# New addresses for the attention buffers, an early load of part of A12, and R21 in front of the other late loads

## The chip, the core and the metric

The kernel runs on one core of one Trainium2 chip. The core has five engines that work side by side and wait for each other through semaphores: TensorE (PE), which multiplies matrices, with its weight loads shown apart as PEld; VectorE (DVE); ScalarE (ACT); GpSimd (POOL), which in this kernel almost only issues DMAs; and SyncE (SP), which issues most of the DMAs. 16 DMA engines move the data between the large memory (HBM) and the core's own memory, which has 128 partitions.

The metric is the device time of one execution in microseconds (us), the median of several. The profile is of one more execution. Its span goes from its first instruction to its last.

## What is computed

Two branches work on the same x of 2048 rows and 1024 columns and are mixed, row by row, by a gate. Cut to what matters:

```python
x = A_x                                                  # (1, 2048, 1024), bf16
g = sigmoid((x * gate_w).sum(-1, keepdims=True))

# A: attention of 32 heads of 32; each row looks at 8 rows: itself and 2, 4, .. 14 before it
qkv = x @ wqkv                                           # 1024 x 3072
logits = einsum("bhsd,bhswd->bhsw", q, kg) * 32**-0.5    # kg, vg: the 8 rows of k, v
attn = softmax(where(mask, logits, -1e9))
a = einsum("bhsw,bhswd->bhsd", attn, vg) @ wo            # heads side by side, 1024 x 1024

# B: a gated feed-forward
h = gelu(x @ w_gate) * (x @ w_up)                        # 1024 x 3584, twice
b = h @ w_down                                           # 3584 x 1024

out = g * a + (1 - g) * b
```

## The kernel before

**Storage.** Nearly all of the core's memory is one tile, `arena`, of 200.5 KB in each partition. Everything in it has an address in KB, written by hand at the head of the file (`R_Q`, `R_O`, `R_BUF`, ...), and different stages use the same addresses one after the other. Semaphore waits are derived from these addresses: an instruction waits for earlier ones that read or wrote the bytes that it touches.

**Stages.** The rows are handled in two halves s of 1024, and each half in two chunks c of 512. First come `units`: products of 512 columns by Strassen-like schemes with seven products instead of eight (methods `p1` to `p4` of `Unit`, all matmuls at L364). The first units make q, k and v, the others gate and up, two pairs of columns at a time; each pair's h is multiplied together (L252, for the last two pairs also by 1 - g at L255) and stored to `h_d` by POOL (L258). `n` is the number of units, about 6 us each. While PE runs the units, DVE also does the attention: background tasks with priorities and wake times (`bg`, `run_bg`) are stepped after each unit with a budget of time. The order of every engine is thus fixed when the program is built.

**Attention output.** `pv_all` goes through the eight blocks of 256 rows in the order `PVO` = 0, 1, 2, 4, 5, 6, 3, 7; i is the turn, a the block. For each it has the weights in `ab_[i % 2]` (4 KB), v in `vb[i % 2]` (4.25 KB), multiplies them (L743) into `prod2` (two buffers of 8 KB), folds the products (L750) into `ob_[i % 2]` (4 KB) and stores that to `o_d` by POOL (L771). The loads of turn i + 1 are issued at the beginning of turn i. The last turn, i = 7, uses the buffers of index 1.

**Down projection.** After the units, `down(s)` multiplies the half's activations A (h of 14 pairs and the 4 tiles of the attention's output: NK = 18 tiles of 1 KB) by R (`w_down` and `wo`), again with seven products in place of eight, and most of these with a second level of the same (`level2`, matmuls at L1025; single-level products at L1050). `A11, A12, A21, A22` are the four parts of A (first digit: which 512 rows; second: which of the two tiles of a pair), `R11 .. R22` those of R, `T1 .. T4` are differences of R made early and kept in HBM (`t_d`). Each lies in one of ten 18 KB buffers, `bufs[k]` from 1 + 18k KB; for s = 0: A12 in buffer 2 (37 to 55 KB), A22 in 3 (55 to 73), A11 in 4, R11 in 5, A21 in 6 (109 to 127), R21 in 7 (127 to 145), T1 in 1 (19 to 37), T2 in 9.

For s = 0 the first half of `down` does, on PE: A11 by R11 (72 matmuls, L1050), A12 by R21 (72, L1050), then `level2` of S and T1 (126, L1025), `level2` of S2 and T2 (126, L1025), A12 by R22 (72, L1050). On DVE, in this order: the rest of the scaling by 1 - g (`scale_task`, L904, 4 tiles an instruction), S = A21 + A22 and AD = A11 - A21 (`comb_task`, L911), the forms L5 and R5 for the first `level2` (L986 and L994, woven), S2 (L911), the forms L6, three instructions of A12 - S2, the forms R6 (L994), and so on.

**The late loads of the first `down`.** `NE_` = 12 is the number of pairs whose h has not been scaled before it is stored, `KX` = 11, the number of tiles of A21 that fit below a buffer of the units at 120 KB. The loads of A are issued in parts:

- `pre_down_0`: A21's tiles 0 to 10; `pre_down_1`: A11's 12 tiles and its o tiles
- `pre_down_2`, called at the end of `pv_all`: A22's 12 tiles, then A12's 12 tiles, and a scaling task for each in this order
- `pre_down_3`, right after it: A21's twelfth tile and its o tiles, the o tiles of A22 and A12, and R21 (two DMAs: 14 tiles of `w_down`, 4 of `wo`, L827)
- `pre_down_4`: the tiles of the last two pairs, issued on POOL (L812)
- T1 and T2 (L830) after the last unit

All but `pre_down_4` go through SP, whose queue is in order: while one DMA waits for its buffer, the ones behind it are not issued. Each DMA takes one of eight semaphore lanes in turn and waits for the DMA eight before it in its lane.

Of the kernel before, what the change touches and what calls it, by code (L numbers as in the profile page):

```python
# [18 lines left out]
NWIN = 8  # L19
# [3 lines left out]
NJ = 4  # L23
SJ = AC // NJ
# [25 lines left out]
R_TF = (92, 100, 108)  # L50
R_TB = (16, 24)
R_S = (16, 24)
R_O = (32, 36)
R_VB = 40
R_AB = 49
R_PROD2 = 57
R_BUF = tuple(1 + 18 * k for k in range(10))
R_U2 = 181
R_QS = 189
# [1 line left out]
KV = AC + HALO  # L61


def _win_ap(src: bass.AP, dims):
    return AP(src.tensor, src.offset, [list(src.ap[0])] + [list(d) for d in dims])
# [3 lines left out]
def kernel(  # L69
# [20 lines left out]
    NT = KT  # L90
    NPAIR = Df // (2 * P)
    NK = NPAIR + NT // 2
    NBLK = S // AC
# [9 lines left out]
    def reg(kb, n):  # L103
        o = int(kb * KB)
        return arena[:, o:o + n]

    def reg3(kb, a, b):
        return reg(kb, a * b).rearrange("p (a b) -> p a b", a=a)

    def reg4(kb, a, b, c):  # L110
        return reg(kb, a * b * c).rearrange("p (a b c) -> p a b c", a=a, b=b)
# [12 lines left out]
    NE_ = NPAIR - 2  # L124
# [10 lines left out]
    with tc.manual_schedule(engines={mybir.EngineType.PE, mybir.EngineType.DVE, mybir.EngineType.Activation,  # L135
# [296 lines left out]
        def bg(gen, prio, wake):  # L432
            t = Task(gen, prio, wake)
            tasks.append(t)
            tasks.sort(key=lambda t_: t_.prio)
            return t
# [134 lines left out]

        qb = [reg3(R_Q + 9 * i, NT, AC) for i in range(2)]
        kb = [reg3(R_Q + 9 * i + 4, NT, KV) for i in range(2)]
        vb = [reg3(R_VB + 4.25 * i, NT, KV) for i in range(2)]
        pr_off = [R_PR + 4 * i for i in range(4)] + [R_PROD + 4 * i for i in range(2)]
        prod = [reg3(o, NWIN, AC) for o in pr_off]
        attn_all = reg3(R_ATTN, NBLK, SC)
        mask = reg3(R_MASK, NWIN, SJ)
        ab_ = [reg4(R_AB + 4 * i, NJ, NWIN, SJ) for i in range(2)]
        ob_ = [reg3(R_O[i], NT, AC) for i in range(2)]  # L580
        prod2 = [reg4(R_PROD2 + 8 * i, 2, NJ, NWIN * SJ) for i in range(2)]

# [133 lines left out]
        def pv_load(a, i):  # L716
            src = w_d[a].rearrange("h j n -> h (j n)")
            nc.sync.dma_start(out=ab_[i % 2].rearrange("p j w s -> p (j w s)"),
                              in_=AP(src.tensor, src.offset,
                                     [[NJ * SC, 32], [0, 4], [1, NJ * SC]]))  # L720
            nc.sync.dma_start(out=vb[i % 2], in_=v_d[:, :, a * AC:a * AC + KV])
# [3 lines left out]
        def pv_all():  # L725
            for k in (0, 1):
                while PVO[k] not in ready:
                    yield None
            pv_load(PVO[0], 0)
            yield None  # L730
            for i, a in enumerate(PVO):
                if i + 1 < NBLK:
                    while PVO[i + 1] not in ready:
                        yield None
                    pv_load(PVO[i + 1], i + 1)
                if i == 0:
                    pv_task[0].prio = 5
                    tasks.sort(key=lambda t_: t_.prio)
                    yield None
                v, ab, o_ = vb[i % 2], ab_[i % 2], ob_[i % 2]  # L740

                def mult(t):
                    TT(out=prod2[(t // 2) % 2][:, t % 2], in0=ab,  # L743
                       in1=_win_ap(v[:, t, HALO:HALO + AC], [[SJ, NJ], [-DIL, NWIN], [1, SJ]]), op=ALU.mult)

                def fold(t, w):
                    pr = prod2[(t // 2) % 2]
                    h = lambda k: pr[:, :, :, k * w * SJ:(k + 1) * w * SJ]
                    out_ = h(0) if w > 1 else o_[:, t:t + 2, :].rearrange("p t (j s) -> p t j s", j=NJ)
                    TT(out=out_, in0=h(0), in1=h(1), op=ALU.add)  # L750

                mult(0)
                yield 1.14
                mult(1)
                yield 1.14
                for t in range(0, NT, 2):
                    nxt = t + 2 < NT
                    if nxt:
                        mult(t + 2)
                        yield 1.14  # L760
                    fold(t, 4)
                    yield 1.14
                    if nxt:
                        mult(t + 3)
                        yield 1.14
                    fold(t, 2)
                    yield 0.68
                    fold(t, 1)
                    yield 0.4
                a0 = a % BPS % 2 * AC  # L770
                nc.gpsimd.dma_start(out=o_d[a // BPS][a % BPS // 2][:, :, a0:a0 + AC], in_=o_)  # L771
            while now[0] < n - 6:
                yield None
            pre_down_2(0)

        def late_forms():
# [24 lines left out]
        bg(spill(0), 4, QE + 2)  # L801
        bg(spill(1), 4, QE + 2)
        pv_task = [bg(pv_all(), 4.2, QE + 3)]

        bufs = [reg3(R_BUF[k], NK, SC) for k in range(10)]
        NH_ = NPAIR

        def load_A(b, s, half, c, i0, i1, with_o, eng=nc.sync):
            for e, (a, z) in enumerate(((i0, min(i1, NE_)), (max(i0, NE_), i1))):
                if z > a:  # L810
                    src = h_d[s][e][:, :, c * SC:(c + 1) * SC].rearrange("p (i two) s -> p i two s", two=2)
                    eng.dma_start(out=b[:, a:z, :], in_=src[:, a - e * NE_:z - e * NE_, half, :])  # L812
            if with_o:
                nc.sync.dma_start(out=b[:, NH_:NK, :], in_=o_d[s][c][:, half * 4:half * 4 + 4, :])
# [10 lines left out]
        def load_R(b, half, nh, i0=0, i1=NK):  # L825
            for sl, src in r_parts(half, nh, i0, i1):
                nc.sync.dma_start(out=b[:, sl, :], in_=src)  # L827

        def load_T(b, k):
            nc.sync.dma_start(out=b, in_=t_d[k - 1][:])  # L830
# [65 lines left out]
        def Bs(s):  # L896
            return {k: bufs[v] for k, v in plan[s].items()}

        def scale_task(b, s, c, ia, ib):
            t0 = s * SUP + c * SC  # L900
            om = omgrep[:, t0:t0 + SC].rearrange("p (o s) -> p o s", o=1)
            for i0 in range(ia, ib, 4):
                i1 = min(i0 + 4, ib)
                TT(out=b[:, i0:i1, :], in0=b[:, i0:i1, :], in1=om.to_broadcast([P, i1 - i0, SC]), op=ALU.mult)  # L904
                yield 0.05 + 0.273 * (i1 - i0)
# [28 lines left out]

        KX = int(R_P5A[0] - R_BUF[6])

        def load_o(s, *names):
            for k in names:
                load_A(Bs(s)[k], s, int(k[2]) - 1, int(k[1]) - 1, 0, 0, True)

        def pre_down_0(s):
            load_A(Bs(s)["A21"], s, 0, 1, 0, KX, False)
            bg(scale_task(Bs(s)["A21"], s, 1, 0, KX), 6, n - 2)

        def pre_down_2(s):
            pd["end"] = True
            for k, c in (("A22", 1), ("A12", 0)):
                load_A(Bs(s)[k], s, 1, c, 0, NE_, False)
                bg(scale_task(Bs(s)[k], s, c, 0, NE_), 7, n)
            if now[0] >= NX0 + 3:  # L950
                pre_down_3(s)

        def pre_down_3(s):
            load_A(Bs(s)["A21"], s, 0, 1, KX, NE_, True)
            load_o(s, "A22", "A12")
            loads(s, "R21")

        def pre_down_4(s):
            B = Bs(s)
# [3 lines left out]
        def loads(s, *names):  # L963
            B = Bs(s)
            for k in names:
                if k[0] == "A":
                    load_A(B[k], s, int(k[2]) - 1, int(k[1]) - 1, 0, NH_, True)
                elif k[0] == "R":
                    load_R(B[k], int(k[1]) - 1, int(k[2]) - 1)
                else:  # L970
                    load_T(B[k], int(k[1]))
# [173 lines left out]
        at(n - 10, lambda: pre_down_0(0))  # L1145
        at(n - 7, lambda: pre_down_1(0))
        at(NX0 + 3, lambda: pd.get("end") and pre_down_3(0))
        def run_last(b):
            now[0] = b
# [72 lines left out]
```

## Time and profile before

| | us |
|---|---|
| median of 3 runs | 735.02 (734.26 to 735.18) |
| the profiled execution | 733.06 |
| its span | 731.2 |
| PE busy | 717.2 |
| DVE busy | 655.0 |
| ACT busy | 317.3 |
| PE idle in all between its matmuls | about 10 |

The busy times are of the whole span, over stages that have different limits: an engine that is 98% busy over all can still stand still at one place. A line of the timeline gives start, length, engine, source line, operation, tiles written and read, and in brackets the engine's idle time before it and what ended it. DMA issues stand at the time at which SP or POOL issued them; a long issue means that the queue took it only after that time. The time from issue to landing comes from the DMA view of a narrow window.

For the stretch around the end of the units these landings are (from the DMA view; issue times from the timeline):

| DMA | KB | issued | us to landing |
|---|---|---|---|
| A22, 12 tiles (SP) | 1536 | 504.86 | 10.3 |
| last block's o_, store (POOL) | 512 | 505.13 | 8.2 |
| A12, 12 tiles (SP) | 1536 | 513.38 | 7.1 |
| A21, twelfth tile (SP) | 128 | 513.99 | 9.0 |
| R21, w_down (SP) | 1792 | 517.11 | 18.6 |
| R21, wo (SP) | 512 | 517.63 | 19.5 |
| T1 (SP) | 2304 | 529.20 | 15.0 |

### The profile page before, as it was taken

To read this page: it belongs to the slowest core of one execution; us is meant where nothing else is said; L and a number is where in the kernel's file an instruction comes from. 1 tells how busy PE (TensorE), PEld (TensorE's weight loads), DVE (VectorE), ACT (ScalarE), POOL (GpSimd) and SP (SyncE) were. 2 spreads that over 40 slices of the span, in tenths; PEclk is the share of its full clock that TensorE was granted. 3 is DMA by queue.
4 is the path that set the end of the run, shared out by engine and by line. 5 is a ranking of instruction groups with operands and counts; after the bars stand their busy time and mean duration, and the time that the engine had idled before them with its cause. 6 is when DMAs were issued, how large, how long until landed. Compare 5 with 4: busy or idle time off the path is not lost. (4 is left out here: it accounts for less than half of the span.)

```text
span 731.2 us, 10391 instructions
## 1 busy us (share of the span) xinstructions
PE 717.2 (98%) x3945; PEld 393.2 (54%) x3945; DVE 655.0 (90%) x703; ACT 317.3 (43%) x570; POOL 114.7 (16%) x212
## 2 busy tenths in 40 slices
PE   8999999999999999999999999999969999999998
PEld 4466666655544444444444444444437766758573
DVE  3699999999999999999999999999779798799944
ACT  4554445444557565555555555555112211232210
POOL 1233445143201210001000000101100011110001
PEclk9999999999999999999999999999989999999999
DMA  9967544287264834443364836533991976965401
GB/s 278 278 180 224 210 139 156 76 282 267 99 211 145 278 113 146 147 144 123 110 203 126 265 121 220 150 137 123 348 363 49 397 254 205 382 276 203 194 22 58
DMA packets 112610, 140.78 MB, mean 193 GB/s; under 512 B 18816, under 2 KB 94752, under 8 KB 111536
## 3 DMA queue, kind: packets, MB, share of 16 engines
q1 hardware_dynamic: 98352, 98.38, 41.7%
q0 software_dynamic: 13920, 41.21, 15.6%
q8 instruction: 31, 0.51, 0.3%
q10 hardware_dynamic: 288, 0.52, 0.3%
q14 instruction: 19, 0.16, 0.1%
HBM read 98.01 MB, written 39.99 MB: 189 GB/s over the span
## 5 line engine op out<-in xcount | busy, mean ns | idle before, releaser
L364 PE MATMUL banks<-arena 128*128 128x512 bf16 x2184 | 474.8, 379 | 1.5 <-DVE arena L401 0.7
L364 PEld LDWEIGHTS <-arena 128*128 128x128 bf16 x2184 | 240.5, 111 | 235.2 <-issue 7.0
L1050 PE MATMUL banks<-arena 128*128 128x512 bf16 x504 | 111.4, 382 | 6.9 <-DMA arena<-in_B_w_down_dram 6.5
L401 DVE TENSOR_TENSOR arena<-banks,arena 128x1024 bf16<-128x1024 f32 x78 | 95.1, 1220 | 13.1 <-PE banks L364 7.9
L387 ACT COPY arena<-banks 128x512 f32<-128x512 f32 x78 | 45.8, 587 | 130.8 <-PE banks L364 130.8
L1025 PE MATMUL banks<-arena 128*128 128x256 bf16 x882 | 97.5, 273 | 0.0
L1025 PEld LDWEIGHTS <-arena 128*128 128x128 bf16 x882 | 86.3, 98 | 11.4 <-issue 0.3
L1050 PEld LDWEIGHTS <-arena 128*128 128x128 bf16 x504 | 49.6, 98 | 66.7 <-DVE arena L911 7.0
L372 ACT CAST arena<-banks 128x512 bf16<-128x512 f32 x102 | 59.6, 584 | 42.4 <-PE banks L364 42.4
L743 DVE TENSOR_TENSOR arena<-arena 128x2048 bf16<-128x2048 bf16 x64 | 76.9, 1218 | 0.5
L596 DVE TENSOR_TENSOR arena<-arena 128x2048 bf16<-128x2048 bf16 x64 | 74.6, 1217 | 0.1
L750 DVE TENSOR_TENSOR arena<-arena 128x2048 bf16<-128x2048 bf16 (+2 forms) x96 | 73.8, 774 | 1.0
L394 ACT COPY banks<-banks 128x512 f32<-128x512 f32 x78 | 44.5, 570 | 21.9 <-PE banks L364 20.1
L258 POOL DMA_DIRECT2D h_d<-arena x28 | 15.1, 541 | 243.5 <-DVE arena L252 213.1
L382 ACT COPY banks<-banks 128x512 f32<-128x512 f32 x78 | 44.9, 576 | 13.6 <-PE banks L364 12.4
L1055 POOL DMA_DIRECT2D out_dram<-arena x28 | 15.2, 541 | 181.4 <-DVE arena L1059 123.7
L994 DVE TENSOR_TENSOR arena<-arena 128x2304 bf16<-128x2304 bf16 x28 | 37.5, 1351 | 5.5 <-DMA arena<-t_d 5.3
L911 DVE TENSOR_TENSOR arena<-arena 128x2048 bf16<-128x2048 bf16 (+1 forms) x40 | 41.9, 1110 | 0.0
L1030 ACT COPY banks<-banks 128x256 f32<-128x256 f32 x42 | 14.9, 356 | 56.7 <-PE banks L1025 56.5
L321 DVE TENSOR_TENSOR arena<-arena 128x1024 bf16<-128x1024 bf16 x60 | 38.6, 685 | 0.5
L252 DVE TENSOR_TENSOR arena<-arena 128x2048 bf16<-128x2048 bf16 x28 | 34.0, 1215 | 5.5 <-ACT arena L372 4.1
L370 ACT ACTIVATE arena<-banks 128x512 bf16<-128x512 f32 x54 | 32.2, 597 | 15.4 <-PE banks L364 15.4
(85 smaller groups left out, 435.1 us busy)
## 6 DMA issues: line engine op xcount, KB each, us to landing
arena<-t_d SPq DMA_DIRECT2D x8, 2304.0 KB, 12.9
h_d<-arena POOLq DMA_DIRECT2D x28, 512.0 KB, 3.6
arena<-in_B_w_down_dram SPq DMA_DIRECT2D x6, 1792.0 KB, 14.2
arena<-h_d SPq DMA_DIRECT2D x7, 1536.0 KB, 10.3
t_d<-arena POOLq DMA_DIRECT2D x36, 256.0 KB, 4.0
arena<-in_B_w_gate_dram SPq DMA_DIRECT2D x15, 512.0 KB, 5.3
arena<-in_B_w_up_dram SPq DMA_DIRECT2D x15, 512.0 KB, 4.8
arena<-in_B_w_down_dram SPq DMA_DIRECT2D x28, 256.0 KB, 7.1
```

The lines of the kernel that those rows point to most:

```text
L364: self.pe = nc.tensor.matmul(ps, lhsT=self.L[form](kt), rhs=rhs[:, kt, :], start=(start and kt == 0), stop=(kt == HK - 1), skip_group_chec ...
L372: nc.scalar.copy(out=o_, in_=i_)
L382: nc.scalar.copy(out=self.Y, in_=self.X)
L387: nc.scalar.copy(out=self.p5s, in_=self.V)
L394: nc.scalar.copy(out=self.Z, in_=self.Y)
L401: TT(out=self.T[:, :, c2s], in0=pair, in1=self.p5s.rearrange("p (o n) -> p o n", o=1).to_broadcast([P, 2, SC]), op=ALU.add)
L596: TT(out=dst, in0=q.rearrange("p (o s) -> p o s", o=1).to_broadcast([P, NWIN, AC]), in1=_win_ap(k, [[-DIL, NWIN], [1, AC]]), op=ALU.mult)
L743: TT(out=prod2[(t // 2) % 2][:, t % 2], in0=ab, in1=_win_ap(v[:, t, HALO:HALO + AC], [[SJ, NJ], [-DIL, NWIN], [1, SJ]]), op=ALU.mult)
L750: TT(out=out_, in0=h(0), in1=h(1), op=ALU.add)
L911: TT(out=f(o_), in0=f(a), in1=f(b), op=op)
L1025: nc.tensor.matmul(c(i, h, j), lhsT=l[:, kt, j * P:(j + 1) * P], rhs=r[:, kt, :], start=False, stop=(kt == KH - 1), skip_group_check=True)
L1050: nc.tensor.matmul(ps, lhsT=L[:, i, j * P:(j + 1) * P], rhs=R[:, i, :], start=(start and q == 0), stop=(q == NK - 1), skip_group_check=not ...
```

## The change

Three things change.

1. The attention's buffers are laid out by turn: those of index 0 lie together, `ob_` 36 to 40, `vb` 40 to 44.25, `ab_` 44.25 to 48.25 KB, and those of index 1 apart from them, `ob_` 32 to 36, `vb` 48.25 to 52.5, `ab_` 52.5 to 56.5. `prod2` begins at 56.5 in place of 57.
2. In the last turn of `pv_all`, which uses index 1, tiles 0 to 10 of A12 (37 to 48 KB) are loaded after the first pair of folds. Only A12's twelfth tile and its o tiles are left for later.
3. After the attention A22 alone is loaded; then come R21, A12's last tile and o tiles, A21's last tile and o tiles, and A22's o tiles. The scaling tasks are created in the order A12, A22.

```diff
-R_O = (32, 36)
-R_VB = 40
-R_AB = 49
-R_PROD2 = 57
+R_O = (36, 32)
+R_VB = (40, 48.25)
+R_AB = (44.25, 52.5)
+R_PROD2 = 56.5
...
-        vb = [reg3(R_VB + 4.25 * i, NT, KV) for i in range(2)]
+        vb = [reg3(R_VB[i], NT, KV) for i in range(2)]
...
-        ab_ = [reg4(R_AB + 4 * i, NJ, NWIN, SJ) for i in range(2)]
+        ab_ = [reg4(R_AB[i], NJ, NWIN, SJ) for i in range(2)]
...
                 for t in range(0, NT, 2):
+                    if i + 1 == NBLK and t == 2:
+                        load_A(Bs(0)["A12"], 0, 1, 0, 0, KX, False)
                     nxt = t + 2 < NT
...
-        def load_o(s, *names):
-            for k in names:
-                load_A(Bs(s)[k], s, int(k[2]) - 1, int(k[1]) - 1, 0, 0, True)
-
...
         def pre_down_2(s):
             pd["end"] = True
-            for k, c in (("A22", 1), ("A12", 0)):
-                load_A(Bs(s)[k], s, 1, c, 0, NE_, False)
+            load_A(Bs(s)["A22"], s, 1, 1, 0, NE_, False)
+            for k, c in (("A12", 0), ("A22", 1)):
                 bg(scale_task(Bs(s)[k], s, c, 0, NE_), 7, n)
             if now[0] >= NX0 + 3:
                 pre_down_3(s)
 
         def pre_down_3(s):
+            loads(s, "R21")
+            load_A(Bs(s)["A12"], s, 1, 0, KX, NE_, True)
             load_A(Bs(s)["A21"], s, 0, 1, KX, NE_, True)
-            load_o(s, "A22", "A12")
-            loads(s, "R21")
+            load_A(Bs(s)["A22"], s, 1, 1, 0, 0, True)
```

The instructions of PE, DVE, ACT and POOL keep their number and order, but for the scaling of A12, which on DVE now stands in front of that of A22, and the addresses of the attention's operands. SP has one DMA more.

## The prediction

> **What bounds the kernel now.** I read the page first, for the engine that sets the end and its idle time, then the waits of SP's queue, then the timeline from 500 to 600 us, then that stretch in windows with clock and DMA, and last the DMA issues in narrow windows, which give each issue's landing.
>
> ```profile
> span 731.2 us, 10391 instructions
> PE 717.2 (98%) x3945; PEld 393.2 (54%) x3945; DVE 655.0 (90%) x703; ACT 317.3 (43%) x570; POOL 114.7 (16%) x212
> ...
> L1050 PE MATMUL banks<-arena 128*128 128x512 bf16 x504 | 111.4, 382 | 6.9 <-DMA arena<-in_B_w_down_dram 6.5
> ```
>
> PE bounds it: 717.2 of 731.2 us busy. Of what is left, one hole is large, 6.5 us before a matmul that waits for a w_down load. The timeline shows the place (start, length, engine, line; idle time before it in brackets):
>
> ```profile
> 504.86 10.07 SPq L812 DMA_DIRECT2D arena<-h_d  x3
> ...
> 517.01 12.25 PE L1050 MATMUL banks<-arena 128*128 128x512 bf16 x56
> ...
> 517.63 11.46 SPq L827 DMA_DIRECT2D arena<-in_A_wo_dram  x1
> ...
> 520.24 7.23 DVE L904 TENSOR_TENSOR arena<-arena,omgrep 128x2048 bf16<-128x2048 bf16 x7
> 527.38 10.37 DVE L911 TENSOR_TENSOR arena<-arena 128x2048 bf16<-128x2048 bf16 x10
> ...
> 535.80 16.99 PE L1050 MATMUL banks<-arena 128*128 128x512 bf16 x72 [6.54 <-DMA arena<-in_B_w_down_dram]
> ...
> 544.29 1.36 DVE L994 TENSOR_TENSOR arena<-arena 128x2304 bf16<-128x2304 bf16 x1 [5.28 <-DMA arena<-t_d]
> ...
> 552.63 27.82 PE L1025 MATMUL banks<-arena 128*128 128x256 bf16 x252
> ...
> 567.18 5.35 DVE L994 TENSOR_TENSOR arena<-arena 128x2304 bf16<-128x2304 bf16 x4
> ...
> 580.29 15.70 PE L1050 MATMUL banks<-arena 128*128 128x512 bf16 x72
> ```
>
> PE ends A11 by R11 at 529.26 (517.01 + 12.25) and waits until 535.80 for R21, whose two pieces SP issued at 517.11 and 517.63. SP was late because the A12 load, second of the three at 504.86, could not be issued until the last block's o_ was stored, which lies in A12's place:
>
> ```profile
> SPq L812 <- DMA o_d<-arena: 7.9, 1, 7.9
> ```
>
> The windows (busy time and count for PE, PEld, DVE, ACT, POOL; then granted clock, DMA share, GB/s) show what came with the hole:
>
> ```profile
> 532.00:536.00 4.00, 0.20 (x1) 0.14 (x2) 4.00 (x6) 0.00 (x0) 0.00 (x0) 0.50 1.15 389
> 536.00:538.40 2.40, 2.40 (x7) 0.82 (x6) 2.40 (x4) 0.00 (x0) 0.00 (x0) 0.50 1.01 425
> 538.40:543.00 4.60, 4.60 (x23) 2.10 (x22) 0.62 (x1) 0.58 (x1) 0.56 (x1) 0.99 1.02 432
> ```
>
> The clock had fallen to half and stayed there until 538.4: the 72 matmuls took 16.99 us against 15.70 for the same 72 at 580.29. DMA is full throughout, so it matters which bytes go first.
>
> **The change, part by part.**
>
> *Layout.* The attention multiplies and folds (L743, L750) keep number, size and order; only addresses move. The first pass over each buffer waits for other early users, but L743 and L750 idled 0.5 and 1.0 us in all, with other tasks beside them: 0, bounds -0.5 and +0.5.
>
> *Early A12.* One more DMA, 11 tiles (1408 KB), in SP's order right behind A11 and its o tiles. It waits for block 6's folds (done 467.3) and that block's o_ store (issued 467.61, POOL). SP is free of the A11 issue at 473.98 (469.56 + 4.42), and nothing follows on SP until 504.86. The nearest row, A21's 1408 KB at 444.89, landed after 8.9 us: about 486, or 490 if the h store at 474.41 shares the engines. Its first reader is at 520. Cost 0: the cover is some 30 us. An h store delayed by 4 us would hold an evacuation tile that is used again only some 25 us later (five tiles, two for each 12 us pair). POOL's issues keep their order.
>
> *R21.* The last block's o_ now lies elsewhere, so the 7.9 us wait is gone, and R21 comes right behind A22 at about 505.4 instead of 517.11; its own wait, for the last matmuls that read the first half's x forms, is over by then: these are three units back, and a unit takes some 6 us. Bytes on SP's queue up to R21's end: A22 1.57 MB, R21 1.84 + 0.52 MB, together 3.93. The hardware queue had moved 1.51 MB by 514.0 while two stores of POOL ran beside it, and then runs at 344 GB/s:
>
> ```profile
> q0 software_dynamic: 277, 1.03, 63.8%
> q1 hardware_dynamic: 509, 0.52, 39.0%
> ...
> DMA packets 1629, 1.72 MB, mean 344 GB/s; under 512 B 25, under 2 KB 1603, under 8 KB 1629
> ```
>
> (The first two are 510 to 514, queue, packets, MB, share; the last is 515 to 520.) So R21 ends at 514.0 + 2.42/0.344 = 521.0 alone. PE needs it at 529.26: the wait is gone, 6.54, and with it the half clock, 16.99 - 15.70 = 1.29. Together 7.83 us at PE.
>
> *What is late next.* Two things lie on DVE, which becomes the tight engine.
>
> First, slack. Of the 252 matmuls from 552.63 (0.1104 each), the 163rd, where the second half's third product begins, needs the first R6 form: 552.63 + 162 x 0.1104 = 570.51. The form is ready at 567.18 + 1.34 = 568.52: slack 1.99. PE now comes 7.83 earlier; DVE, which is unbroken from 517.83 on but for the 5.28 before T1, comes at most 5.28 earlier. PE waits 7.83 - 5.28 - 1.99 = 0.56. This needs T1 by 537.67 + 1.35 = 539.0. Ahead of T1 stand 1.44 MB less than before (the early tiles): behind R21 0.26 MB of single tiles, 1.57 MB of o tiles and T1's 2.36 MB on SP, with POOL's four h loads and a store, 1.57 MB. At the 396 GB/s of 526 to 530, 5.76 MB take 14.5 us from 521.0: 535.6, and some 2 us for the slowest DMA engine. Just in time. T2 waits in its lane for R21's first piece and is read only at 567.18 - 5.3.
>
> The single tile of A21 and the three o loads, which R21 has passed, end with POOL's transfers by 521.0 + 3.40/0.396 = 529.6, A12's o tiles first. PE reads those after twelve matmuls, 529.3 + 12 x 0.218 = 531.9, and DVE reads A21's and A22's in the fourth addition of S, after 530.5: 0, with 1 to 2 us of cover.
>
> Second, A12's twelfth tile. It goes behind R21, and DVE now scales A12 first: the third L904 of the run, at 520.24 + 2 x 1.14 = 522.5, needs it, and everything on DVE queues behind it: A22's scaling, S, AD and all forms. Before, A22 stood there, landed 10.3 us after 504.86. The tile's 0.13 MB end at 514.0 + 2.55/0.344 = 521.4 if POOL is quiet. POOL's h loads (1.05 MB, first bytes around 520) are not quiet: beside POOL, SP's queue moved 0.52 MB in 4 us, 0.13 MB/us. By 520.0 it has 2.06 of 2.55 MB done; 0.49/0.13 = 3.8 us more: 523.8. Landing follows the last bytes by about 1 us (A22: 1.51 of 1.57 MB moved at 514.0, landed 515.13). So 522.4 to 524.8, and up to 526.4 if SP is again held for 11.46 us by the wo issue and the tile takes the 9.0 us that A21's single tile took. DVE's wait: 0 to 3.9, and I take 1.8, near the contended reading. Each us of it reaches PE at R6, since the slack is spent.
>
> Sum: 7.83 - 0.56 - 1.8 = 5.5 us. The profiled execution has a span of 731.2 and 733.06 in all (1.9 around it): 725.7 and 727.6. It lies 2.0 under the median of 735.02; the same 5.5 off the median gives **729.5**.
>
> After 580 DVE waits for PE again (3.13 and 1.27 us at L1014), so the gain is carried, not given back: R22, T3 and T4 are issued as PE and DVE free their buffers, and R22 landed 7.6 us before its use.
>
> [...]
>
> **The rivals.**
>
> *The tile is in time.* POOL's loads start late enough (they began 4 to 5 us after 515.63). Gain 7.83 - 0.56 = 7.3: 727.7. Against it: 521.4 plus 1 is already at the edge.
>
> *The wait brings the half clock back.* A stop of 0.56 + 1.8 = 2.4 us at R6 is as long as the idle time after which the clock fell at 531.6. The low spell lasted 6.8 us, of which 4.2 idle; half of it, 3.4 us, at half speed costs 1.7. Gain 3.8: 731.2; with the tile at 526.4, 7.83 - 4.46 - 1.7 = 1.7: 733.3.
>
> *R21 in front starves DVE, slower.* Place: the third L904. Every us after 522.5 is a us at PE, and with the half clock the gain is used up from a landing at 522.5 + 7.83 - 0.56 - 1.7 = 528.1. At 531 it loses 2.9: 737.9. For it: before, R21's pieces took 18.6 and 19.5 us from issue to landing. Against it: 10 us of these lay behind A12, A21 and three o loads, which now come after.
>
> *It doesn't do what it says:* R21 is issued early but lands after 535 as before. It would need 30 us for 3.93 MB. About 735.
>
> **How the numbers follow.** Forecast (728.3 to 730.8): 0.46. Tile in time (727 to 728.3): 0.24. Half clock or a tile after 525.5 (730.8 to 733.5): 0.20. No change: 0.05. Slower: 0.05. A measurement of this kernel tells 0.2%, 1.5 us, from no change. Faster 0.90, same 0.05, slower 0.05. The range leaves out a tenth at each end: 727.0 to 732.8; the likeliest case's own is 728.3 to 730.8.
>
> **What would show it.** R21 issued near 505.4 and landed near 522; no PE idle before its 72 matmuls, which take 15.7 at full clock; a wait on DVE at the third scaling of the run, and PE idle of that size plus 0.6 in the second group of L1025. Wrong if T1, not the tile, holds DVE, or if the hole comes back at R21.

## The result, and the profile after

The changed kernel takes 732.35 us (median of 6 runs, 731.21 to 733.33) against 734.33 for the kernel before beside it: ratio 0.997, interval 0.9957 to 0.9983. That is 2.0 us faster, where 5.5 had been forecast. The profiled execution took 731.21, its span is 729.4 against 731.2.

The hole before R21 is gone, and another one has opened 30 us later. From the page and from the groups of the profile after (source lines have moved: L904 is L906, L911 L913, L986 L985, L994 L993, L1025 L1024, L1050 L1049, L812 L814, L827 L829; in the runs further down they differ by a line or two again):

```profile
span 729.4 us, 10330 instructions
PE 714.7 (98%) x3883; PEld 393.0 (54%) x3945; DVE 655.1 (90%) x703; ACT 317.2 (43%) x570; POOL 114.7 (16%) x212
```

```profile
L1049 PE MATMUL banks<-arena 128*128 128x512 bf16 x492 | 109.3, 379 | 1.0 <-ACT arena L1106 0.4
L1024 PE MATMUL banks<-arena 128*128 128x256 bf16 x882 | 100.3, 277 | 3.7 <-DVE arena L993 3.7
```

L1049 idles 1.0 us before it in place of 6.9, and no longer for a load of w_down; L1024, which had no idle time at all, now has 3.7, and its mean has risen from 273 to 277 ns. (A few matmul records are missing from this trace; the counts of the program are the same.) The timeline has the places:

```profile
504.63 0.53 SPq L814 DMA_DIRECT2D arena<-h_d  x1
...
505.26 0.88 SPq L829 DMA_DIRECT2D arena<-in_B_w_down_dram  x1
...
506.19 7.67 SPq L829 DMA_DIRECT2D arena<-in_A_wo_dram  x1
...
513.90 2.48 SPq L814 DMA_DIRECT2D arena<-h_d  x1
...
516.79 27.79 PE L1049 MATMUL banks<-arena 128*128 128x512 bf16 x126
...
520.01 2.36 DVE L906 TENSOR_TENSOR arena<-arena,omgrep 128x2048 bf16<-128x2048 bf16 x2
...
525.37 4.97 DVE L906 TENSOR_TENSOR arena<-arena,omgrep 128x2048 bf16<-128x2048 bf16 x5 [3.00 <-DMA arena<-h_d]
...
544.42 18.00 PE L1024 MATMUL banks<-arena 128*128 128x256 bf16 x162
...
564.68 5.35 DVE L993 TENSOR_TENSOR arena<-arena 128x2304 bf16<-128x2304 bf16 x4
566.08 12.64 PE L1024 MATMUL banks<-arena 128*128 128x256 bf16 x90 [3.67 <-DVE arena L993]
```

Read it downwards. R21 is issued at 505.26 and 506.19, 11 to 12 us earlier than before, and PE runs from A11 by R11 into A12 by R21 without a stop: one row of 27.79 us. A12's last tile is issued behind R21 at 513.90 and lands 11.4 us later, at 525.3. DVE has scaled two groups of A12 and stands still for 3.00 us until then; everything after it is late, the first R6 form is ready only at 566.0, and PE stops after its 162nd matmul, exactly where the slack had been worked out, for 3.67 us. The windows show the second part of the price (columns as before):

```profile
562.00:566.00 4.00, 0.42 (x4) 0.22 (x3) 4.00 (x4) 0.00 (x0) 0.00 (x0) 0.84 1.19 446
566.00:571.50 5.50, 5.42 (x26) 3.75 (x26) 5.40 (x6) 0.74 (x2) 0.00 (x0) 0.50 0.50 214
571.50:578.00 6.50, 6.50 (x61) 5.78 (x60) 2.18 (x4) 3.40 (x8) 0.00 (x0) 1.00 0.66 227
```

The granted clock falls to half during the stop (0.84 as a mean means 1.3 of 4 us) and stays there until 571.5. The 90 matmuls from 566.08 took 12.64 us; 90 of the 252 in the profile before take 27.82 x 90/252 = 9.94. So the low clock cost 2.70, about half of the 5.5 us of it in which PE worked.

The sum with measured terms is 7.83 - 3.67 - 2.70 = 1.5 us. The trace has the same: the matmuls of A12 by R22 begin at 578.56 and not at 580.29, 1.7 earlier, of which 0.2 were there already at 516.79 against 517.01.

### The profile page after: what moved, and what is told of

Read it like the earlier page. It is cut to its first block, busy times and chain, and to the rows that moved or that the text cites. A ratio compares the mean times of both kernels' runs of the same rounds, so it can differ in the third digit from the quotient of the medians.

```text
span 729.4 us, 10330 instructions
## 1 busy us (share of the span) xinstructions
PE 714.7 (98%) x3883; PEld 393.0 (54%) x3945; DVE 655.1 (90%) x703; ACT 317.2 (43%) x570; POOL 114.7 (16%) x212
## 5 line engine op out<-in xcount | busy, mean ns | idle before, releaser
L1049 PE MATMUL banks<-arena 128*128 128x512 bf16 x492 | 109.3, 379 | 1.0 <-ACT arena L1106 0.4
L1024 PE MATMUL banks<-arena 128*128 128x256 bf16 x882 | 100.3, 277 | 3.7 <-DVE arena L993 3.7
L1024 PEld LDWEIGHTS <-arena 128*128 128x128 bf16 x882 | 87.3, 99 | 16.8 <-issue 4.2
L1049 PEld LDWEIGHTS <-arena 128*128 128x128 bf16 x504 | 49.2, 98 | 59.1 <-issue 0.6
L743 DVE TENSOR_TENSOR arena<-arena 128x2048 bf16<-128x2048 bf16 x64 | 77.0, 1219 | 0.5
L750 DVE TENSOR_TENSOR arena<-arena 128x2048 bf16<-128x2048 bf16 (+2 forms) x96 | 73.8, 775 | 1.0
L394 ACT COPY banks<-banks 128x512 f32<-128x512 f32 x78 | 44.5, 570 | 21.9 <-PE banks L364 20.1
L913 DVE TENSOR_TENSOR arena<-arena 128x2048 bf16<-128x2048 bf16 (+1 forms) x40 | 41.9, 1110 | 0.0
L985 DVE TENSOR_TENSOR arena<-arena 128x2304 bf16<-128x2304 bf16 x28 | 37.5, 1352 | 0.5
```

The source lines that it names most:

```text
L743: TT(out=prod2[(t // 2) % 2][:, t % 2], in0=ab, in1=_win_ap(v[:, t, HALO:HALO + AC], [[SJ, NJ], [-DIL, NWIN], [1, SJ]]), op=ALU.mult)
L913: TT(out=f(o_), in0=f(a), in1=f(b), op=op)
L985: TT(out=o_, in0=a, in1=b_, op=op)
L1024: nc.tensor.matmul(c(i, h, j), lhsT=l[:, kt, j * P:(j + 1) * P], rhs=r[:, kt, :], start=False, stop=(kt == KH - 1), skip_group_check=True)
L1049: nc.tensor.matmul(ps, lhsT=L[:, i, j * P:(j + 1) * P], rhs=R[:, i, :], start=(start and q == 0), stop=(q == NK - 1), skip_group_check=not ...
```

## The experiments

Each starts from the changed kernel; the diffs are cut to the lines that matter. Ratios are to the kernel before, run beside it on the same chip.

**A12's tile in front of R21.**

```diff
         def pre_down_3(s):
+            load_A(Bs(s)["A12"], s, 1, 0, KX, NE_, False)
             loads(s, "R21")
-            load_A(Bs(s)["A12"], s, 1, 0, KX, NE_, True)
+            load_A(Bs(s)["A12"], s, 1, 0, 0, 0, True)
```

> A12's twelfth tile is issued in front of R21 instead of behind it; all else as in the changed kernel. Theory (the tile behind R21 holds DVE for 3.00 us at the third scaling, this makes PE stop 3.67 us before the first R6 form, and the stop halves the clock): the tile lands before 520, DVE's wait of 3.00 is gone, R21 lands some 0.4 us later than 520.88 and 523.65 and still in time, PE's stop is 3.67 - 3.00 = 0.67 us, the clock stays full. Gain over the kernel before 7.83 - 0.67 = 7.2 us: 727 us, ratio 0.990. Rival (DVE has too much work here whatever the tile does): PE's stop stays over 2 us and the clock falls, 730 us or more.

729.79 us, ratio 0.9931 (0.9907 to 0.9956). The tile is in time, and DVE goes on to the next thing behind R21, A21's single tile, and waits there:

```profile
520.69 6.90 DVE L906 TENSOR_TENSOR arena<-arena,omgrep 128x2048 bf16<-128x2048 bf16 x6
...
529.60 0.42 DVE L906 TENSOR_TENSOR arena<-arena,omgrep 128x512 bf16<-128x512 bf16 x1 [2.01 <-DMA arena<-h_d]
```

```profile
565.78 11.65 PE L1025 MATMUL banks<-arena 128*128 128x256 bf16 x90 [2.69 <-DVE arena L994]
```

PE stops 2.69 us at R6, and the 90 matmuls behind it take 11.65 us in place of 9.94: the clock fell too, the mean granted clock is 0.59 from 566 to 570. The stop and the time are those of the rival, but not its reason: DVE does not have too much work, it waits 2.01 us for a load. The theory had the right chain and missed the next link: I had named one late tile where others behind R21 are late too.

**A22 scaled first.**

```diff
-            for k, c in (("A12", 0), ("A22", 1)):
+            for k, c in (("A22", 1), ("A12", 0)):
```

> Loads as in the changed kernel, but DVE scales A22 before A12, as the kernel before did. Theory (DVE's order, not the DMA order by itself, makes the wait): A22 landed 516.37, so DVE starts at 520 without a wait, and comes to the twelfth tile after five instructions, at 520.0 + 5 x 1.14 = 525.7, when it has landed (525.34). PE's stop 0.7 us, clock full, 727 us, ratio 0.990, the same as with the tile in front of R21. Rival (R21 in front starves later readers too): the wait moves to the o tiles, the stop stays over 2 us, 730 us.

729.47 us, ratio 0.9919 (0.9887 to 0.9951). In this execution A12's tile landed 21.9 us after A22's issue, 1.2 later than in the profile after with the same loads (20.7), and DVE waited twice, 0.77 for it and 0.94 for A21's tile. PE's stop was 2.48 us:

```profile
565.82 11.47 PE L1024 MATMUL banks<-arena 128*128 128x256 bf16 x90 [2.48 <-DVE arena L993]
```

So the order on DVE moves the wait and makes it shorter, 1.71 us in all against 3.00; neither side had the place right, the rival had the size. This one line also takes the ratio from 0.997 to 0.9919, and the two intervals do not touch: a good part of what the changed kernel loses goes with its order of scaling and not with R21's place. One of the four executions took 727.58 at a mean granted clock of 1.000, the others 729.15 to 729.80 at 0.997 or 0.998. In that one the clock stayed full, and the time is near the theory's 727; the profile is of one of the others.

**The old order of the late loads.** This keeps the layout and the early load, and takes R21 from the front.

```diff
         def pre_down_3(s):
-            loads(s, "R21")
-            load_A(Bs(s)["A12"], s, 1, 0, KX, NE_, True)
+            load_A(Bs(s)["A12"], s, 1, 0, KX, NE_, False)
             load_A(Bs(s)["A21"], s, 0, 1, KX, NE_, True)
             load_A(Bs(s)["A22"], s, 1, 1, 0, 0, True)
+            load_A(Bs(s)["A12"], s, 1, 0, 0, 0, True)
+            loads(s, "R21")
```

(A22 is scaled first here too.)

> The new layout and the early load alone: the late loads go in the order of the kernel before (single tiles and o tiles first, R21 last), and A22 is scaled first. Theory (the 7.9 us wait of SP for the o_ store was what made R21 late, and its place in the order matters little): the last load in this order ended at 531.07 in the changed kernel, so R21's two pieces land about 530 and 531; PE is ready at 529.0 and stops 1 to 2 us, too little to halve the clock; no stop at R6. Gain 7.83 - 1.5 = 6.3 us: 728 us, ratio 0.991. Rival (the place in front is what brings the gain): PE stops 4 us or more before its A12 matmuls, with half clock, 731 us or more.

726.19 us, ratio 0.9883 (0.9858 to 0.9907): 6 us better than the changed kernel. The timeline:

```profile
530.57 15.70 PE L1050 MATMUL banks<-arena 128*128 128x512 bf16 x71 [1.02 <-DMA arena<-in_A_wo_dram]
546.10 27.83 PE L1025 MATMUL banks<-arena 128*128 128x256 bf16 x252
```

R21's pieces landed at 530.4 and 531.9, where 530 and 531 had been worked out. PE stops 1.02 us for the first of them (the line names the wo load, but that landed only after PE had gone on), at full clock afterwards (15.70 for the 72), and nowhere else: DVE never waits for a load, and the 252 matmuls run in one row. The stop is as the theory has it, the time 2 us below its 728. R21's place in front is not what removes the hole.

**The layout alone.** The loads come in the order of the run above, but without the early load: A12's twelve tiles come after A22, as in the kernel before. A22 is scaled first.

```diff
-                    if i + 1 == NBLK and t == 2:
-                        load_A(Bs(0)["A12"], 0, 1, 0, 0, KX, False)
...
         def pre_down_3(s):
+            load_A(Bs(s)["A12"], s, 1, 0, 0, NE_, False)
+            load_A(Bs(s)["A21"], s, 0, 1, KX, NE_, False)
+            load_A(Bs(s)["A21"], s, 0, 1, 0, 0, True)
+            load_A(Bs(s)["A22"], s, 1, 1, 0, 0, True)
+            load_A(Bs(s)["A12"], s, 1, 0, 0, 0, True)
             loads(s, "R21")
-            load_A(Bs(s)["A12"], s, 1, 0, KX, NE_, True)
-            load_A(Bs(s)["A21"], s, 0, 1, KX, NE_, True)
-            load_A(Bs(s)["A22"], s, 1, 1, 0, 0, True)
```

> The new layout alone: A12's 12 tiles are loaded after A22 again, late loads and scaling in the order of the kernel before; only the o_ buffer of the last turn no longer lies in A12's place, so that SP has no wait of 7.9 us. Theory (the 1.44 MB taken out of the full stretch are worth as much as the wait): in the run with the old order and the early load R21 landed at 530.43 and 531.91; 1.44 MB more in front at 344 GB/s are 4.2 us, so 534.6 and 536.1; PE stops about 5.5 us and the clock falls: 733 us, ratio 0.998. Rival (SP's wait was the cause of it all): R21 lands near 531, PE stops under 2 us, 727 us.

732.78 us, ratio 0.9971 (0.996 to 0.9983).

```profile
533.79 17.39 PE L1049 MATMUL banks<-arena 128*128 128x512 bf16 x72 [4.76 <-DMA arena<-in_B_w_down_dram]
```

R21's first piece is issued at 515.26 instead of 517.11 and lands at 533.7 instead of 535.7, as the theory had it. SP no longer waits 7.9 us for the o_ store: it issues A12 at 505.25 instead of 513.38. But its next issue, A21's single tile, is held up for 6.72 us:

```profile
506.23 6.72 SPq L812 DMA_DIRECT2D arena<-h_d  x1
```

So most of the old wait was time that the bytes in front needed anyway. Against the run above only the early load is missing, so most of the gain comes from the 1.44 MB that it moves out of the full stretch. (It was not run on the old layout, where the last turn's buffers lie in its place.)

**POOL's loads behind SP's.**

```diff
-                load_A(B[k], s, int(k[2]) - 1, int(k[1]) - 1, NE_, NH_, False, nc.gpsimd)
+                load_A(B[k], s, int(k[2]) - 1, int(k[1]) - 1, NE_, NH_, False)
```

> The changed kernel, but the four loads of the last two pairs' h (256 KB each) go behind the late loads on SP's queue instead of POOL's own queue. Theory (R21's bytes and POOL's loads beside them both hold A12's twelfth tile back): with POOL quiet until its h store at 520.66 the hardware queue runs at its full rate of 344 GB/s after 514, and the tile lands at about 522.4 instead of 525.34 to 527.20; DVE's wait there is 0 to 0.5 us. Rival (the tile is late by its place in the queue alone, POOL's loads do not matter): it lands after 525 as before. The h loads themselves will be late, so PE may wait for A11's last two tiles at about 527; the time tells nothing, the landing does.

One execution, 728.0. R21's second piece landed 16.6 us after its issue (17.5 in the changed kernel), A12's tile 8.6 (11.4), at 523.8:

```profile
523.87 4.97 DVE L906 TENSOR_TENSOR arena<-arena,omgrep 128x2048 bf16<-128x2048 bf16 x5 [0.76 <-DMA arena<-h_d]
```

The wait is 0.76 against 3.00, a little over the 0 to 0.5 that had been worked out: POOL's loads beside R21 make most of it. As expected, the h loads are now late themselves; PE stopped 2.03 us for them, until 530.09, with no half clock in the stretch (the mean granted clock of the execution is 1.000). There is no stop at R6, since PE itself comes later by more than the 0.76 + 0.67 that would be missing there.

**Both single tiles in front, o tiles behind.**

```diff
         def pre_down_3(s):
+            load_A(Bs(s)["A12"], s, 1, 0, KX, NE_, False)
+            load_A(Bs(s)["A21"], s, 0, 1, KX, NE_, False)
             loads(s, "R21")
-            load_A(Bs(s)["A12"], s, 1, 0, KX, NE_, True)
-            load_A(Bs(s)["A21"], s, 0, 1, KX, NE_, True)
+            load_A(Bs(s)["A12"], s, 1, 0, 0, 0, True)
+            load_A(Bs(s)["A21"], s, 0, 1, 0, 0, True)
```

> Both single tiles (A12's and A21's) in front of R21, the three o loads behind it, A12 scaled first. With A12's tile alone in front the wait moved to A21's tile (2.01 us, landed 529.58). Theory (whatever DVE reads next behind R21 comes too late): the o tiles land about 529.5, 531 and 532.3, the fourth addition of S is due at 530.6 and waits 1 to 2 us; PE stops 1.5 to 2.5 us at R6, with half clock for 3.4 us if it is over 2: 728 to 730 us, ratio 0.992 to 0.994. Rival (only single tiles were the trouble): no DVE wait over 0.5, PE stop 0.7, 726.5 us.

726.44 us, ratio 0.989 (0.9873 to 0.9906). The wait is once more at the next reader, the o tiles (landed 531.5), and it is shorter:

```profile
531.61 4.10 DVE L913 TENSOR_TENSOR arena<-arena 128x2048 bf16<-128x2048 bf16 x4 [0.74 <-DMA arena<-o_d]
```

```profile
564.05 9.98 PE L1026 MATMUL banks<-arena 128*128 128x256 bf16 x90 [1.41 <-DVE arena L995]
```

The second line shows the 90 matmuls after a stop of 1.41 us: 9.98 us, so at full clock (1.00 in the windows from 560 to 570). That a stop over 2 us would bring the half clock back was an estimate, and this stop lies under it. The place is the theory's, but wait and stop lie under its ranges (1 to 2 and 1.5 to 2.5), and the time is the rival's.

**Fewer additions in front of R6.** Three of DVE's A12 - S2 additions stand before the R6 forms in the first half; here one.

```diff
             if not last:
-                take(rest, 3)
+                take(rest, 1)
             run(forms_R(B["R6"], B["T2"]), rest)
```

> The changed kernel, but one instead of three of the A12 - S2 additions of DVE stands in front of the R6 forms in the first half; DVE's wait of 3.00 us stays. Theory (PE stops as long as the first R6 form is late, and a stop of 1.4 us doesn't halve the clock): the form is ready 2.28 us earlier, PE's stop is 3.67 - 2.28 = 1.4, clock full: gain 7.83 - 1.4 = 6.4 us, 728 us, ratio 0.991, so that 2.7 us of this come from the clock alone. If the clock falls in spite of it: 730.5 us.

728.87 us, ratio 0.9921 (0.9893 to 0.9949). The number that was to be held fixed did not hold: the tile landed 22.6 us after A22's issue in the profiled execution, and DVE waited 4.87 us.

```profile
527.22 4.97 DVE L906 TENSOR_TENSOR arena<-arena,omgrep 128x2048 bf16<-128x2048 bf16 x5 [4.87 <-DMA arena<-h_d]
```

```profile
565.67 11.53 PE L1024 MATMUL banks<-arena 128*128 128x256 bf16 x90 [3.27 <-DVE arena L993]
```

PE's stop was 3.27 = 4.87 + 0.67 - 2.28, with half clock for 3.4 us. The median lies between the two numbers, and the four executions fall on both: 728.00 and 728.02 at a mean granted clock of 1.000, as the theory has it with the clock full, and 729.73 and 730.17 at 0.998, near the 730.5 with the clock fallen. The chain from tile to stop is borne out; that a stop of 1.4 us keeps the clock is shown by the run before this one.

**A combination.** Single tiles, A21's and A22's o tiles, R21, A12's o tiles; A22 scaled first; two additions in front of R6.

```diff
         def pre_down_3(s):
+            load_A(Bs(s)["A12"], s, 1, 0, KX, NE_, False)
+            load_A(Bs(s)["A21"], s, 0, 1, KX, NE_, False)
+            load_A(Bs(s)["A21"], s, 0, 1, 0, 0, True)
+            load_A(Bs(s)["A22"], s, 1, 1, 0, 0, True)
             loads(s, "R21")
-            load_A(Bs(s)["A12"], s, 1, 0, KX, NE_, True)
-            load_A(Bs(s)["A21"], s, 0, 1, KX, NE_, True)
-            load_A(Bs(s)["A22"], s, 1, 1, 0, 0, True)
+            load_A(Bs(s)["A12"], s, 1, 0, 0, 0, True)
...
-                take(rest, 3)
+                take(rest, 2)
```

> Single tiles, A21's and A22's o tiles, then R21, then A12's o tiles; A22 scaled first; two instead of three of the A12 - S2 additions in front of R6. In the run with the old order and the early load (726.19) PE stopped 1.02 us for R21 and nowhere else; here R21 has 0.52 MB less in front, 1.3 to 1.5 us, so PE's stop before R21 is 0 to 0.4 us, the first R6 form is 1.14 us earlier and there is no stop there: 726 us, ratio 0.988 to 0.989. Rival (A12's o tiles behind R21 now hold PE at the twelfth matmul): a stop of 1 us or more there, 727 us.

725.03 us, ratio 0.9872 (0.9857 to 0.9887), the lowest median, though its interval overlaps with those of the old order and of both single tiles in front. R21 landed at 528.3 and 529.8, A12's o tiles at 531.0, and PE does not stop:

```profile
516.84 27.79 PE L1051 MATMUL banks<-arena 128*128 128x512 bf16 x128
544.47 27.82 PE L1026 MATMUL banks<-arena 128*128 128x256 bf16 x252
```

The whole hole with its low clock was worth 7.83 us by the profile before; 734.76 to 725.03 is 9.7 by medians, and the spans of the profiled executions, 731.2 and 723.0, differ by 8.2. Most of the difference between these two is that the profiled execution of the kernel before, 733.06, lies 1.7 under this median; what the rest is, is not shown.

## Why the prediction was wrong

**The hole before R21** was sized rightly: 6.54 us and 1.29 of half clock are gone. That the bytes in front of R21, not its wait alone, made it late is shown by the layout alone, which still stops 4.76.

**The slack at R6** was the right place, and nearly the right size. In five runs PE's stop there is DVE's wait plus 0.67, to 0.1, where 0.56 had been worked out.

| run | DVE waits for loads | PE stop at R6 | half clock after it |
|---|---|---|---|
| changed kernel | 3.00 | 3.67 | 6.8 |
| A12's tile in front | 2.01 | 2.69 | 3.4 |
| A22 scaled first | 0.77 + 0.94 | 2.48 | 3.4 |
| one addition in front of R6 | 4.87 | 3.27 (2.28 earlier by the edit) | 3.4 |
| both tiles in front | 0.74 | 1.41 | none |

The last column is worked out from the mean granted clock of windows. From 564 to 566 and from 566 to 570 this is 0.87 and 0.64 with A22 scaled first, 0.86 and 0.64 with one addition, and 1.00 and 1.00 with both tiles in front. With A12's tile in front, where it is 1.00 and 0.59, the 90 matmuls give 2 x (11.65 - 9.94) = 3.4.

**Two steps failed: the third term, "DVE's wait: 0 to 3.9, and I take 1.8", and the clock that hangs on it, for which the sum has no term.** The sum came out 4.0 us too high: 1.2 of this is the wait (3.00 for 1.8), 0.1 the slack, and 2.7, the larger part, the half clock.

*The wait.* It was 3.00, and 4.87 in another execution with the same loads, over the upper bound. The count of bytes was good at first: 1.50 MB of SP's queue had moved by 514 (1.51 assumed) and 3.51 MB by 520 (3.57). After that, two things were priced wrongly, in opposite directions. Beside POOL's loads the queue was to move 0.13 MB in a us; it moved 0.54 MB from 520 to 522, as POOL's loads had only begun (0.18 MB in these 2 us), and by 522 it had moved as many bytes as A22, R21 and the tile have together (1.57 + 2.36 + 0.13 = 4.06 MB):

```profile
q1 hardware_dynamic: 3963, 4.05, 74.7%
```

(504.5 to 522; queue, packets, MB, share.) The landing was to follow these bytes by about 1 us, and it followed by 3.3, at 525.3. That the contended reading, 524.8, is only 0.5 off is luck: the two errors nearly cancel. From 522 to 525, before the tile was there, the profile after has:

```profile
DMA packets 407, 1.11 MB, mean 368 GB/s; under 512 B 63, under 2 KB 162, under 8 KB 407
...
q0 software_dynamic: 204, 0.66, 63.0%
q1 hardware_dynamic: 203, 0.45, 41.9%
```

Of the 407 packets 245 (407 - 162) are of 4 KB; POOL's queue has at most 204 of them, so at least 41 belong to SP's o loads, which stand behind the tile. Parts of the queue had passed the tile by, while some of its 1 KB rows were still to come. That POOL's loads are what holds them is borne out by the one execution without them, where DVE waits 0.76 and the landing followed the bytes by 1.3 us (4.05 MB at 522.5, landed at 523.8); that it is some of the 16 DMA engines that lag is only argued from these packets, and the trace does not tell the engines apart.

*The clock* was a rival, "the wait brings the half clock back", with a fifth of the chance and 1.7 us. It happened, and cost 2.70: the low spell lasted 6.8 us, where the rival had counted half of that, 3.4, as an estimate. Its first time, 731.2, was nearer to the 732.35 than the forecast. The stop that I forecast myself, 2.4 us, was as long as the time after which the clock had fallen in the profile before, and I still counted it as full clock in the sum. The line of that profile, where PE had stopped at 529.26, has 0.94 as the mean clock of 3 us, so the clock fell about 2.4 us after the stop:

```profile
529.00:532.00 3.00, 0.27 (x2) 0.00 (x0) 3.00 (x4) 2.07 (x5) 0.00 (x0) 0.94 1.09 371
```

That a stop of this length costs no clock is not shown by any run: the nearest are one of 2.03 us, which left it full, and one of 2.48, in the run with A22 scaled first, after which it was at half for 3.4 us.

**The edits at nothing** held. The early load was issued at 473.60 and landed at 486.4, 34 us before its reader. T1 landed at 537.5, where 535.6 and some 2 us had been worked out, and did not hold DVE. The 2 us were an estimate; in the profile before, at the end of T2, the DMA share is 1.05 until 545.4 and 0.66, 0.55 and 0.13 in the next three windows of 0.6 us. The layout cost nothing: L743 and L750 idle 0.5 and 1.0 us as before.

**What each part of the change is worth**, by the ratios: the layout alone 0.9971; with the early load 0.9883; with the third part as well 0.997. Two parts gain 1.2%, and the third gives most of it back. The third is itself two edits: R21 in front with A22 scaled first stands at 0.9919, so by these ratios R21's place costs about 0.4% (the intervals of 0.9883 and 0.9919 overlap) and scaling A12 first about 0.5%. The old order of loads with A12 scaled first was not run.

## What to carry to other kernels

Here the DMA share was 1.02 to 1.08 from 514 to 538 in the changed kernel, and the order of transfers chose who was late: DVE waited 3.00 us for A12's tile behind R21, 2.01 for A21's tile with A12's in front, and 0.74 for the o tiles with both in front. Before one is moved to the front, list the first reader of each transfer that it passes and how much slack that reader's engine has; here R21 had 1 us to gain over its old place and passed two single tiles and three o loads. In each of the runs with R21 in front of A21's and A22's o tiles, DVE, which had no slack, waited for one or two of these. Taking bytes out of the full stretch, as the early load does, had no such other side here.

Price a stall together with the clock: stops of 1.02, 1.41 and 2.03 us cost their length here; one of 2.69 brought 1.7 on top (the 90 matmuls took 11.65 in place of 9.94), one of 3.67 brought 2.7, and one of 4.76 again 1.7 (17.39 in place of 15.70).

## What the hardware did that I had not expected

Stops of 1.02, 1.41 and 2.03 us left the clock full; stops of 2.48, 2.69, 3.27 and 4.76 brought one low spell of 3.4 us, and those of 3.67 and 6.54 one of 6.8. So in these runs the length of the spell did not follow the length of the stop. What sets the two spells of 6.8 apart in these traces is that PE stood still for another 1.4 and 4.2 us after the clock had fallen; in the spells of 3.4 it did so for less than 0.4 us. Nor did the clock fall at a fixed time: by the mean clock of the windows it fell 2.1 us (A22 scaled first), 2.3 (changed kernel), 2.4 (kernel before), 3.0 (one addition), 3.6 (A12's tile in front) and 5.0 us (layout alone) after PE had stopped, in the last two only after PE had taken up work again. This is the layout alone, where PE stops at 529.03 and goes on at 533.79:

```profile
529.00:533.80 4.80, 0.04 (x2) 0.04 (x2) 4.80 (x6) 1.83 (x4) 0.00 (x0) 1.00 1.13 364
533.80:537.40 3.60, 3.60 (x9) 1.30 (x10) 3.60 (x4) 0.00 (x0) 0.00 (x0) 0.53 1.05 437
```

No stop between 2.03 and 2.48 us was measured, nor whether a stop of one length does the same in every execution.

A tile of 128 KB, issued behind R21 at nearly the same time, landed 20.7, 21.9 and 22.6 us after A22's issue in three executions with the same loads. The six runs of the changed kernel cover 2.1 us, the four of the combination, which waits for nothing there, 0.7. That the spread of the landings makes the spread of the times is likely but not shown: the mean granted clock is 0.994 or 0.995 in all six, and their landings were not profiled but for one.
